# A second MLP's first product over pairs of token tiles by Strassen's scheme, with its token mixes made by scaled stores and accumulating DMAs

## The chip, the cores and the metric

The program runs on one core of a Trainium2 chip. The metric is the device time of one execution in microseconds, as the median of repeated runs.

## What is computed

```python
X = np.fft.fft(np.fft.fft(x, axis=1), axis=2).real   # x: (4, 3072, 256)
h = X @ w_in                                          # (256, 2048)
x = np.maximum(0.01 * h, h) @ w_out                   # (2048, 256): the first MLP
x_prev = the token before, zeros for the first of a batch
xk = mu_k * x + (1.0 - mu_k) * x_prev
xr = mu_r * x + (1.0 - mu_r) * x_prev
k = np.maximum(xk @ w_k, 0.0)                         # w_k: (256, 1024): the first product
v = k * k @ w_v                                       # w_v: (1024, 256)
out = v / (1.0 + np.exp(-(xr @ w_r)))                 # w_r: (256, 256): the gate
```

All is float32. Each matrix product is made of three TensorE products of split operands: with w = wh + wl and x = xh + xl, the kernel adds wh·xh, wl·xh and wh·xl (names that end in h and l, the high and the low part). "High" is a ScalarE copy into the type float32r, "low" is a VectorE subtraction of the high part from the value.

## The kernel before

The tokens of the 4 batches are cut into 24 tiles of 512 (`W`), 6 a batch. A tile's token is a column; the 256 features lie on 128 partitions in two halves, `h` = 0 and 1.

**Transform and first MLP**, to about 889 us of the profiled execution: for each batch the Fourier transform is made from folded input and cosine tables (`fft_mm`), then the loop over `NF` = 16 units of 128 hidden columns for each of 3 pairs of tiles calls `step` (L605): on TensorE `mm_b`, `mm_a` (six products into one bank) and `outmm` (L520, twelve products `o`); on ScalarE and VectorE the evacuation `ev`, `g`, `gh`, `gl`. Two tiles come out at a time, and `flush` copies them out of PSUM (`yo`) and stores them to HBM (`y`), 512 KB by one DMA. In between, the weights of the second MLP are converted in nine pieces (`w2_piece`, five steps each).

**Second MLP**, from about 889 us: for each tile, `load_tile` fetches the tile (`xa`) and, in one to three column runs, the tokens before it (`xb`), by DMAs from SyncE's queue. `prep` makes the mixes: ScalarE scales `xb` (L701, `mt`), VectorE adds the scaled `xa` (L702, `mx`), and `hi_lo` splits the sum (`mh`, `ml`). For each of `NK` = 8 blocks `f` of 128 hidden columns, `k_mm` (L945) makes the first product, six products into a bank `kps` (two feature halves, three split terms each); `k_ev` makes relu and square (`rl` on ScalarE, `k` on VectorE), `k_split` splits the result (`k2h`, `k2l`), and `v_mm` (L986) adds six products to the two banks `v` of the tile. Twice a tile, the gate's six products `rps` (L995) and a sigmoid (`sig`, L997) stand in between. At a tile's end VectorE multiplies `sig` and `v` (`o`, L1004), and the result is stored.

The order on each engine is the order in which the Python program records instructions: there is no scheduler. Each engine takes its list in order; a DMA is issued by the queue of SyncE or, for accumulating ones, of GpSimd (POOL), in order as well. PSUM has eight banks: four of the pool `ps_s` go round, four of `ps_o` hold `v` for two tiles.

Of the kernel before, what the change touches and what calls it, by code (L numbers as in the profile page):

```python
# [17 lines left out]
P = 128  # L18
# [84 lines left out]
def fft_mlp_kernel(ctx, tc, xs, x7, x8, x87, tb, tbs, alt, ce, so, mu, w_in, w_out, w_k, w_v, w_r, out):  # L103
# [5 lines left out]
    yd = [[dram.tile([P, 2, M], F32, name=f"y{b}_{s}") for s in range(2)] for b in range(B)]  # L109
# [279 lines left out]
    omu = misc.tile([P, 4], F32, name="omu")  # L389

# [131 lines left out]

    def flush(b, t, po):
        end = b == B - 1 and t == NT - 1
        for s in range(2):
            if end:
                at = yd[b][s][:, :, t * W:(t + 1) * W]
                yo = stage.tile([P, 2, W], F32, tag="st", bufs=3, name="yo") if s == 0 else None
                for h in range(2):
                    half = yo[:, h] if s == 0 else stage.tile([P, W], F32, tag="h", bufs=2, name="yh")  # L530
                    act_copy(half, po[s][h])
                    if s:
                        Q.dma_start(at[:, h], half)
                if s == 0:
                    Q.dma_start(at, yo)
                continue
            yo = work.tile([P, 2, W], F32, tag="yo", bufs=2, name="yo")
            for h in range(2):
                act_copy(yo[:, h], po[s][h])
            Q.dma_start(yd[b][s][:, :, t * W:(t + 1) * W], yo)  # L540
# [96 lines left out]
    kept = [[dram.tile([P, 2, 256], F32, name=f"w2_{n}{x}") for x in "hl"] for n in range(n_early)]  # L637

# [13 lines left out]
    def w2_piece(n):  # L652
        z = {"fp": stage, "ft": "f"}
        nm, src, at = sources[n]

        def load():
            z["st"] = load_f64(src, 2, 256)

        def parts():
            if n < n_early:  # L660
                return (stage.tile([P, 2, 256], F32R, tag="r", bufs=3, name="wh"),
                        stage.tile([P, 2, 256], F32R, tag="h", bufs=2, name="wl"))
            return at(w2[nm + "h"]), at(w2[nm + "l"])

        head, one, two, low, add, four, five = split_steps(z, 2, 256, parts)

        def last():
            five()
            if n < n_early:
                for k, t in zip(kept[n], z["p"]):  # L670
                    Q.dma_start(k, t.bitcast(F32))
            if n + 1 < len(sources):
                w2_load[n + 1]()
        return load, [lambda: (head(), one()), two, lambda: (low(), add()), four, last]

    w2_load, w2_steps = [], []
    for n in range(len(sources)):
        a, c = w2_piece(n)
        w2_load.append(a)
        w2_steps += c  # L680
# [3 lines left out]
    def load_tile(ti):  # L684
        b, i = tiles[ti]
        s, t = divmod(i, NT)
        p = w2["xp"] if ti == 0 else w2["p2"]
        x = p.tile([P, 2, W], F32, tag="xa", name="xa")
        xprev = p.tile([P, 2, W], F32, tag="xb", name="xb")
        Q.dma_start(x, yd[b][s][:, :, t * W:(t + 1) * W])  # L690
        for s, q, c, n in runs_before(TOKENS[i]):
            if s is None:
                V.memset(xprev[:, :, c:c + n], 0.0)
            else:
                Q.dma_start(xprev[:, :, c:c + n], yd[b][s][:, :, q:q + n])
# [24 lines left out]


    def prep_early(x, xprev, r):
        z = {}

        def mix(h):
            t = stage.tile([P, W], F32, tag="h", bufs=2, name="mt")
            z[h] = stage.tile([P, W], F32, tag="f", bufs=2, name="mx")
            A.activation(t, xprev[:, h], ACTF.Copy, scale=omu[:, h:h + 1])
            V.scalar_tensor_tensor(z[h], x[:, h], mut[:, h:h + 1], t, op0=ALU.mult, op1=ALU.add)

        def split(h):
            if h == 0:
                r["k"] = [stage.tile([P, 2, W], F32R, tag="st", bufs=3, name=f"m{n}") for n in "hl"]
            hi_lo(r["k"][0][:, h], r["k"][1][:, h], z[h])
        return [lambda: mix(0), lambda: mix(1), lambda: split(0), lambda: split(1)]

    tiles = [(b, i) for b in range(B) for i in range(2 * NT)]
    loaded, ready = {}, {}

    def do_prep(ti):  # L740
        x, xprev = loaded.pop(ti)
        ready[ti] = {}
        steps = prep(x, xprev, ready[ti])
        return steps if ti > 0 else prep_early(x, xprev, ready[ti]) + steps[3:]
# [108 lines left out]
    for b in range(B):  # L853
# [5 lines left out]
        for ti in range(0 if b else 1, NT):  # L859
# [3 lines left out]
            for u in range(NF):  # L863
# [9 lines left out]
                step(x, nx)  # L873
                for kb, kind, k_u in ((b, "Pe", pe_u), (b, "Qe", qe_u), (b + 1, "Po", po_u), (b + 1, "Qo", qo_u)):
# [41 lines left out]
                if len(w2_steps) > 5 * (len(sources) - n_early):  # L916
                    if po_u <= i < po_u + 5 or (b > 0 and i < 5):
                        w2_steps.pop(0)()
                elif b == B - 1 and i > 7 and w2_steps and i % 3:
                    w2_steps.pop(0)()  # L920
                if b == B - 1:
                    if i == 33:
                        Q.dma_start(mut, mu)
                    if i == 36:
                        V.tensor_scalar(omu, mut, -1.0, 1.0, op0=ALU.mult, op1=ALU.add)
                        loaded[0] = load_tile(0)
                    if i == 39:
# [20 lines left out]
    def k_ev(ps, r, k2):  # L948
# [3 lines left out]
    def small(tag, dt=F32):  # L952
        return stage.tile([P, W], dt, tag=tag, bufs={"r": 3}.get(tag, 2), name="e" + tag)

    early = []
    for f in range(2):
        early.append([ps_s.tile([P, 512], F32, tag="s", name="ps"), small("h"), small("f")])
        k_mm(early[f][0], f, ready[0]["k"])
        if f == 0:
            step(None, None)  # L960
        k_ev(*early[f])
    kk0 = (small("r", F32R), small("r", F32R))
    hi_lo(*kk0, early[0][2])
    stage_out(hist.pop(0))
    wo.release()
# [4 lines left out]


    p2 = w2["p2"] = ctx.enter_context(tc.tile_pool(name="p2", bufs=2))
    p2.tile([P, 16], F32, tag="pad", bufs=1, name="pad3")

    NB = D // P

    def v_mm(f, kk, vps, end):
        hi, lo = kk
        ws = ((w2["vh"], hi), (w2["vl"], hi), (w2["vh"], lo))
        order = [(i, m, slice(0, W)) for i in range(3) for m in range(NB)]  # L980
        if f == NK - 1:
            halves = [slice(0, W // 2), slice(W // 2, W)] if end else [slice(0, W)]
            order = [(i, m, c) for m in range(NB) for c in (halves if m == NB - 1 else [slice(0, W)]) for i in range(3)]
        for i, m, c in order:
            w, x = ws[i]
            T.matmul(vps[m][:, c], w[:, f, m * P:(m + 1) * P], x[:, c], start=(f == 0 and i == 0),  # L986
                     stop=(f == NK - 1 and i == 2), skip_group_check=c.start > 0)

    def r_mm(xr, sig, m):
        hi, lo = xr  # L990
# [6 lines left out]
        A.activation(sig[:, m], ps, ACTF.Sigmoid)  # L997

    def finish(ti, vps, sig):
        o = p2.tile([P, NB, W], F32, tag="o", name="o")  # L1000
        end = ti == len(tiles) - 1
        for m in range(NB):
            for c in [slice(0, W // 2), slice(W // 2, W)] if end and m == NB - 1 else [slice(0, W)]:
                V.tensor_tensor(o[:, m, c], sig[:, m, c], vps[m][:, c], op=ALU.mult)  # L1004
                if end:
                    Q.dma_start(out[ti, :, m, c], o[:, m, c])
        if ti < len(tiles) - 1:
            Q.dma_start(out[ti], o)
# [140 lines left out]
```

## Time and profile before

| | us |
|---|---|
| median of 3 runs | 1481.06 (1481.03 to 1481.28) |
| profiled execution | 1480.61 |
| its span, first to last instruction | 1478.8 |
| TensorE busy | 1462.4 (99%) |
| VectorE busy | 1008.7 (68%) |
| ScalarE busy | 892.6 (60%) |

The span is 1.8 us shorter than the profiled execution's own time. Busy shares are read together with the chain that ended last: an engine that is busy all the time and carries the chain sets the end; idle time of the others costs nothing. TensorE's instructions overlap: an entry of 389 ns does not mean that the next begins 389 ns later.

### The profile page before, as it was taken

The numbers are of one execution on the slowest core, as the hardware profiler recorded it, in microseconds if no ns is written. First come the engines' busy times: TensorE is split into PE (matmuls) and PEld (weight loads), VectorE is DVE, ScalarE is ACT, GpSimd is POOL, SyncE is SP. The second block draws the span as 40 slices with busy tenths as digits, with TensorE's granted clock in tenths as the row PEclk, the third lists the DMA queues.
The fourth block names the chain that finished last, engine by engine and source line by source line (L and its number), as shares of the span: only waits on it lengthen the run. The fifth ranks groups of instructions, "written<-read, shape, count | busy, mean of one in ns | idle before, by whom it ended". The sixth has DMA issues, their size and how long they took to land.

```text
span 1478.8 us, 17665 instructions
## 1 busy us (share of the span) xinstructions
PE 1462.4 (99%) x6463; PEld 1203.6 (81%) x6463; DVE 1008.7 (68%) x1410; ACT 892.6 (60%) x1473; POOL 124.0 (8%) x145
## 2 busy tenths in 40 slices
PE   6999999999999999999999999999999999999998
PEld 3788888888888888888888888888888888888887
DVE  7886667666676666666667666666666666666665
ACT  4776566656666565665666667555555555556563
POOL 2333100132000222000000000000000000000000
PEclk9999999999999999999999999999999999999999
DMA  8867133654132653142230103212121212121200
GB/s 306 234 162 150 36 100 108 199 105 93 36 122 91 193 103 54 36 158 93 79 80 0 57 1 129 67 62 71 58 71 57 72 58 72 57 72 57 72 29 29
DMA packets 88609, 134.23 MB, mean 91 GB/s; under 512 B 31374, under 2 KB 51863, under 8 KB 84938
## 3 DMA queue, kind: packets, MB, share of 16 engines
q1 hardware_dynamic: 73258, 86.50, 18.5%
q0 software_dynamic: 15264, 46.60, 12.8%
q8 instruction: 50, 0.82, 0.2%
q14 instruction: 37, 0.30, 0.1%
HBM read 105.20 MB, written 27.89 MB: 90 GB/s over the span
## 4 chain that ended last, share of the span: by engine, by line
PE 98%; DVE 1%; ACT 0%; DMA 0%; issue 0%; SPq 0%; POOL 0%; DVEq 0%; POOLq 0%; ACTq 0%
PE o L520 35%; PE v L986 18%; PE kps L945 17%; PE ps L497 9%; PE ps L509 9%; PE rps L995 4%; PE wps L402 1%; PE cps L451 1%; PE dps L553 1%; DMA cet<-in_ce 0%; PE f0Po L310 0%; PE f0Pe L310 0%; PE f2Pe L310 0%; PE f1Pe L310 0%; PE f0Qe L310 0%; PE f3Pe L310 0%
## 5 line engine op out<-in xcount | busy, mean ns | idle before, releaser
L592 DVE SCALAR_TENSOR_TENSOR g<-ev,ps 128x512 f32<-128x512 f32 x192 | 131.6, 685 | 191.9 <-PE ps L509 191.2
L949 ACT ACTIVATE rl<-kps 128x512 f32<-128x512 f32 x190 | 113.5, 597 | 227.8 <-PE kps L945 227.7
L580 DVE TENSOR_TENSOR gl<-g,gh 128x1024 fp32r<-128x1024 f32 x192 | 235.0, 1224 | 4.2 <-ACT gh L129 4.2
L129 ACT ACTIVATE gh<-g 128x1024 fp32r<-128x1024 f32 x192 | 202.7, 1056 | 51.7 <-PE o L520 50.5
L950 DVE SCALAR_TENSOR_TENSOR k<-kps,rl 128x512 f32<-128x512 f32 x190 | 131.3, 691 | 146.2 <-ACT rl L949 145.6
L520 PE MATMUL o<-gh,uoh 128*128 128x512 f32 x768 | 211.9, 390 | 1.0 <-ACT gh L129 1.0
L520 PE MATMUL o<-gl,uoh 128*128 128x512 f32 x768 | 211.2, 389 | 0.1
L520 PE MATMUL o<-gh,uol 128*128 128x512 f32 x768 | 211.1, 389 | 0.0
L132 ACT ACTIVATE g<-ps 128x512 f32<-128x512 f32 x192 | 114.3, 595 | 150.1 <-DVE g L592 149.2
L520 PEld LDWEIGHTS o<-gh,uoh 128*128 128x128 f32 x768 | 144.1, 188 | 32.0 <-ACT gh L129 1.5
L520 PEld LDWEIGHTS o<-gl,uoh 128*128 128x128 f32 x768 | 144.1, 188 | 30.4 <-DVE gl L580 0.5
L520 PEld LDWEIGHTS o<-gh,uol 128*128 128x128 f32 x768 | 144.2, 188 | 30.0
L502 DVE SCALAR_TENSOR_TENSOR ev<-cb,w,ps 128x512 f32<-128x512 f32 x192 | 143.1, 746 | 5.0 <-PE ps L497 2.7
L136 DVE TENSOR_TENSOR k2l<-k,k2h 128x512 fp32r<-128x512 f32 x190 | 129.5, 682 | 0.5 <-ACT k2h L129 0.5
L986 PE MATMUL v<-k2l,wvh 128*128 128x512 f32 x383 | 121.7, 389 | 0.0
L986 PE MATMUL v<-k2h,wvh 128*128 128x512 f32 x383 | 121.7, 389 | 0.0
L986 PE MATMUL v<-k2h,wvl 128*128 128x512 f32 x383 | 121.7, 388 | 0.0
L132 ACT ACTIVATE g<-g 128x512 f32<-128x512 f32 x192 | 119.8, 624 | 1.6 <-DVE g L592 1.6
L129 ACT ACTIVATE k2h<-k 128x512 fp32r<-128x512 f32 x190 | 118.4, 623 | 0.0
L945 PE MATMUL kps<-ml,wkh 128*128 128x512 f32 x380 | 117.1, 389 | 0.0
L945 PE MATMUL kps<-mh,wkh 128*128 128x512 f32 x380 | 117.1, 389 | 0.0
L945 PE MATMUL kps<-mh,wkl 128*128 128x512 f32 x380 | 117.0, 389 | 0.0
(396 smaller groups left out, 2183.1 us busy)
## 6 DMA issues: line engine op xcount, KB each, us to landing
xa<-y SPq DMA_DIRECT2D x24, 512.0 KB
y<-yo SPq DMA_DIRECT2D x23, 512.0 KB
out_dram<-o SPq DMA_DIRECT2D x23, 512.0 KB
tab_a<-in_tbs POOLq DMA_DIRECT2D x8, 1158.0 KB, 6.4
tab_b<-in_tbs POOLq DMA_DIRECT2D x8, 1158.0 KB, 5.6
tab_c<-in_tbs POOLq DMA_DIRECT2D x6, 1158.0 KB, 6.1
tab_d<-in_tbs POOLq DMA_DIRECT2D x6, 1158.0 KB, 6.6
pm<-in_xs POOLq DMA_DIRECT2D x54, 128.0 KB, 3.2
```

The source lines that it names most:

```text
L129: A.activation(o, i, ACTF.Copy)
L132: A.activation(o, i, ACTF.Prelu, alpha=0.01)
L136: V.tensor_tensor(lo, src, hi.bitcast(F32), op=ALU.subtract)
L497: T.matmul(x["ps"], l[:, f], r, start=(i == 0), stop=(i == 2))
L502: V.scalar_tensor_tensor(x["ev"], x["cb"], w128[:, u:u + 1], x["ps"], op0=ALU.mult, op1=ALU.add)
L509: T.matmul(x["ps"], l[:, f], r, start=False, stop=(i == 2), skip_group_check=True)
L520: T.matmul(po[s][h], w[:, u % HF, h * P:(h + 1) * P], g[:, s], start=(u == 0 and i == 0), stop=(u == NF - 1 and i == 2))
L580: V.tensor_tensor(gl, x["g"], x["gh"].bitcast(F32), op=ALU.subtract)
L592: V.scalar_tensor_tensor(x["gt"][:, 1], x["ev"], 2.0, x["ps"], op0=ALU.mult, op1=ALU.subtract)
L945: T.matmul(ps, w[:, k, sl], x[:, k], start=(i == 0), stop=(i == 5))
L950: V.scalar_tensor_tensor(k2, ps, 0.0, r, op0=ALU.max, op1=ALU.mult)
L986: T.matmul(vps[m][:, c], w[:, f, m * P:(m + 1) * P], x[:, c], start=(f == 0 and i == 0), stop=(f == NK - 1 and i == 2), skip_group_check=c ...
```

## The change

For 22 of the 24 tiles the first product is made for two tiles, A and B, and two blocks f0 and f1 at once. With the feature halves 1 and 2 and the weights' 128x128 blocks w(half, block), four results c11 (tile A, f0), c12 (B, f0), c21 (A, f1), c22 (B, f1) need eight block products. Strassen's scheme, in Winograd's form, needs seven (`operands`, products 1 to 7), with three of them accumulated onto the same bank `kx` one after the other: it is read after each (`p1`, `u2`, `u4`, last `c12`). One `superstep` makes the four results; four supersteps (`j` = 0 to 3) make a pair, eleven pairs make 22 tiles. Tiles 0 and 1 keep the old product.

- The combined weights (`ws`, 4 blocks for each two f) are made in two further steps of each of the four pieces of w_k (`combine`, `sum_split`), kept in HBM (`sums`) and loaded back (L1220).
- The combined tokens (`t13`, `t24`) and their splits are made once a pair by `pair_steps`, in the slots `more` of the pair before.
- The mixes are no longer computed in the second MLP. In the first MLP, after each unit, `scale_one` (L526) writes a finished tile's half scaled by mu or 1 - mu to one of four HBM arrays, 256 KB by one DMA: eight stores for each two halves of 128 features of a tile, where one store of 512 KB was. `load_mix` loads the first array's tile by a plain DMA and adds the shifted tokens' runs by accumulating DMAs from GpSimd's queue (L730). The last two tiles are kept unscaled (`yraw`) and scaled in pairs 1 to 4.
- c11 and c21 get relu and square on ScalarE (`eh`, `er`), c22 on VectorE alone, c12 as before. What is left of c21, `late`, is recorded in the next superstep.

```diff
+    def scaled(b, s, t, h, k, y, new):
+        z = new()
+        A.activation(z, y, ACTF.Copy, scale=muts[k][:, h:h + 1])
+        Q.dma_start(yd[k][b][s][:, h, t * W:(t + 1) * W], z)
...
     def flush(b, t, po):
...
-            Q.dma_start(yd[b][s][:, :, t * W:(t + 1) * W], yo)
+            for k in range(4):
+                for h in range(2):
+                    scales.append((b, s, t, h, k, yo[h]))
...
                 step(x, nx)
+                scale_one()
+                if u % 4 == 3:
+                    scale_one()
...
+    def load_mix(dst, k, ti, E=Q):
         b, i = tiles[ti]
         s, t = divmod(i, NT)
...
+        E.dma_start(dst, yd[k][b][s][:, :, t * W:(t + 1) * W])
         for s, q, c, n in runs_before(TOKENS[i]):
...
+            if s is not None:
+                G.dma_start(dst[:, :, c:c + n], yd[k + 1][b][s][:, :, q:q + n], accum_op=ALU.add)
...
+    def operands(z, j):
+        kw = lambda k, f: [w2["k" + x][:, k, f * P:(f + 1) * P] for x in "hl"]
+        sw = lambda n: [w[:, j, n] for w in (wsh, wsl)]
+        half = lambda nm, h: [x[:, h] for x in z[nm]]
+        f0, f1 = 2 * j, 2 * j + 1
+        return {1: (kw(0, f0), half("b", 0)), 2: (kw(1, f0), half("b", 1)), 3: (sw(3), z["b22"]), 4: (kw(1, f1), half("t24", 1)),
+                5: (sw(0), half("t13", 0)), 6: (sw(1), half("t24", 0)), 7: (sw(2), half("t13", 1))}
+
+    def product(ps, wx, start):
+        (wh, wl), (xh, xl) = wx
+        for i, (w, x) in enumerate(((wh, xh), (wl, xh), (wh, xl))):
+            T.matmul(ps, w, x, start=(start and i == 0), stop=(i == 2), skip_group_check=not start)
...
+    def superstep(p, j, z, ta, tb, gates, prep):
...
+        X = bank("kx")
+        product(X, w[1], True)
+        Y = bank("ky")
+        product(Y, w[2], True)
+        p1 = piece("p1", 1)
+        act_copy(p1, X)
+        c = piece("c", 3)
+        V.tensor_tensor(c, p1, Y, op=ALU.add)
+        run_late()
+        if pend:
+            v_mm(pend.pop(0))
+        product(X, w[6], False)
+        Z = bank("kz")
+        product(Z, w[7], True)
+        u2 = piece("u2", 1)
+        act_copy(u2, X)
+        c11["k"] = k_act(c)
+        split_hi(c11)
+        if pend:
+            v_mm(pend.pop(0))
+        product(X, w[5], False)
+        u4 = piece("u4", 1)
+        act_copy(u4, X)
+        split_lo(c11)
+        more(1)
+        for g in gates[:1]:
+            gate_mm(*g)
+        c = piece("c", 3)
+        V.tensor_tensor(c, u4, Z, op=ALU.add)
+        c22["k"] = k_vec(c)
+        if pend:
+            v_mm(pend[0], 0)
+        more(1)
+        for g in gates[:1]:
+            gate_ev(*g)
+        split_hi(c22)
+        product(X, w[3], False)
+        if pend:
+            v_mm(pend.pop(0), 1)
+        split_lo(c22)
+        more(1)
+        product(Z, w[4], False)
+        r = small("h")
+        A.activation(r, X, ACTF.Relu)
+        c12["k"] = small("r")
+        V.scalar_tensor_tensor(c12["k"], X, 0.0, r, op0=ALU.max, op1=ALU.mult)
+        v_mm(c11)
+        split_hi(c12)
+        c = piece("c", 3)
+        V.tensor_tensor(c, u2, Z, op=ALU.add)
+        split_lo(c12)
+        more(9)
...
+            prep[1] += [bh, bl, b22h, b22l]
+            prep[2] += [t13, th, tl, t2]
+            prep[3] += [t4, uh, ul, lambda: r_hi(b), lambda: r_lo(b)]
...
+                prep[j][at:at] = [lambda: scale_one(lambda: small("f"))] * (1 + j // 3)
+            superstep(p, j, za, ta, tb, gates[j:j + 1], prep[j])
```

How the order moves on TensorE, in the middle of the second MLP. Before, one block f of one tile: six products into `kps`, then six for `v`:

```order
L945 MATMUL kps<-mh,wkh 128x512 x2
L945 MATMUL kps<-mh,wkl 128x512 x2
L945 MATMUL kps<-ml,wkh 128x512 x2
L986 MATMUL v_9936<-k2h,wvh 128x512
L986 MATMUL v_9937<-k2h,wvh 128x512
L986 MATMUL v_9936<-k2h,wvl 128x512
L986 MATMUL v_9937<-k2h,wvl 128x512
L986 MATMUL v_9936<-k2l,wvh 128x512
L986 MATMUL v_9937<-k2l,wvh 128x512
```

Now, the beginning of a superstep, from the last of the three instructions of product 1 to product 6:

```order
L1083 MATMUL kx<-bl,wkh 128x512
L1083 MATMUL ky<-bh,wkh 128x512
L1083 MATMUL ky<-bh,wkl 128x512
L1083 MATMUL ky<-bl,wkh 128x512
L1002 MATMUL v_10042<-k2h,wvh 128x512
L1002 MATMUL v_10043<-k2h,wvh 128x512
L1002 MATMUL v_10042<-k2h,wvl 128x512
L1002 MATMUL v_10043<-k2h,wvl 128x512
L1002 MATMUL v_10042<-k2l,wvh 128x512
L1002 MATMUL v_10043<-k2l,wvh 128x512
L1083 MATMUL kx<-t24h,wsh 128x512
```

The bank `kx` is written again nine instructions after product 1 was complete, and ScalarE has to have copied it (`p1`) by then. The whole program has 6276 matrix instructions where it had 6408: 132 fewer.

On ScalarE, before, around two blocks f with the mixes (`mt`, `mh`) between:

```order
L701 ACTIVATE mt<-xb,omu 128x512
L949 ACTIVATE rl<-kps 128x512
L129 ACTIVATE k2h<-k_9387 128x512
L129 ACTIVATE mh<-mx 128x1024
L949 ACTIVATE rl<-kps 128x512
L129 ACTIVATE k2h<-k_9410 128x512
```

Now, from the end of a superstep j = 3 into j = 0 of the next pair:

```order
L1163 ACTIVATE eh<-kx 128x512
L129 ACTIVATE k2h<-er 128x512
L129 ACTIVATE rh<-st 128x1024
L129 ACTIVATE p_11300<-kx 128x512
L1092 ACTIVATE eh<-c 128x512
L1093 ACTIVATE er<-eh 128x512
L129 ACTIVATE k2h<-er 128x512
L129 ACTIVATE u_11325<-kx 128x512
L1092 ACTIVATE eh<-c 128x512
L1093 ACTIVATE er<-eh 128x512
L129 ACTIVATE k2h<-er 128x512
L129 ACTIVATE u_11349<-kx 128x512
```

The copies of `kx` (`p1`, `u2`, `u4`) stand behind chains of three instructions on one value (`eh` relu, `er` square, `k2h` high part), and `p1` of j = 0 stands behind the 1024 wide `rh`.

On GpSimd's queue, which issued nothing in the second MLP, these loads now stand, here a part of one pair (`m` for the first product, `st` for the gate):

```order
L730 DMA m<-y_1_0_69 128x2x255
L730 DMA m<-y_1_0_69 128x2x1
L730 DMA m<-y_1_0_69 128x2x256
L730 DMA st<-y_1_0_85 128x2x255
L730 DMA st<-y_1_0_85 128x2x1
L730 DMA st<-y_1_0_85 128x2x256
```

Each row is one accumulating DMA of one run of columns; a pair has ten of them on average.

## Rows read from the trace of the kernel before

**Rows 1.** the page: busy time by engine; then the chain's shares by engine and line.

```profile
PE 1462.4 (99%) x6463; PEld 1203.6 (81%) x6463; DVE 1008.7 (68%) x1410; ACT 892.6 (60%) x1473; POOL 124.0 (8%) x145
...
PE 98%; DVE 1%; ACT 0%; DMA 0%; issue 0%; SPq 0%; POOL 0%; DVEq 0%; POOLq 0%; ACTq 0%
PE o L520 35%; PE v L986 18%; PE kps L945 17%; PE ps L497 9%; PE ps L509 9%; PE rps L995 4%; PE wps L402 1%; PE cps L451 1%; PE dps L553 1%; DMA cet<-in_ce 0%; PE f0Po L310 0%; PE f0Pe L310 0%; PE f2Pe L310 0%; PE f1Pe L310 0%; PE f0Qe L310 0%; PE f3Pe L310 0%
```

**Rows 2.** busy time by stretch: PE, PEld, DVE, ACT, POOL busy (instructions), clock, DMA share, GB/s.

```profile
0.00:60.00 60.00, 47.80 (x177) 30.12 (x178) 46.97 (x85) 33.79 (x61) 19.75 (x22) 1.00 0.89 291
...
420.00:630.00 210.00, 210.00 (x940) 174.59 (x939) 142.24 (x188) 127.50 (x208) 29.89 (x37) 1.00 0.41 105
...
890.00:900.00 10.00, 10.00 (x45) 8.04 (x44) 6.76 (x10) 7.01 (x12) 0.00 (x0) 1.00 0.95 314
900.00:1100.00 200.00, 200.00 (x884) 165.43 (x883) 137.53 (x199) 120.75 (x199) 0.00 (x0) 1.00 0.19 64
...
1470.00:1479.00 9.00, 4.60 (x24) 3.73 (x22) 2.13 (x4) 0.88 (x2) 0.00 (x0) 0.99 0.17 58
```

**Rows 3.** the chain in order of time, second MLP: start us, us, what.

```profile
1150.89 1.36 PE kps L945 x6
1152.25 1.36 PE v L986 x6
```

**Rows 4.** groups by form: name, shapes xcount | busy us, mean ns | idle before, releasers.

```profile
L945 PE MATMUL kps<-mh,wkh 128*128 128x512 f32 x380 | 117.1, 389 | 0.0
```

**Rows 5.** timeline near the end: start us, us, engine, line, instruction [idle before].

```profile
1462.43 0.60 ACT L949 ACTIVATE rl<-kps 128x512 f32<-128x512 f32 x1 [1.60 <-PE kps L945]
1462.92 0.62 ACT L129 ACTIVATE k2h<-k 128x512 fp32r<-128x512 f32 x1
1463.06 0.69 DVE L950 SCALAR_TENSOR_TENSOR k<-kps,rl 128x512 f32<-128x512 f32 x1 [1.43 <-ACT rl L949]
...
1463.67 0.68 DVE L136 TENSOR_TENSOR k2l<-k,k2h 128x512 fp32r<-128x512 f32 x1
...
1471.24 0.61 PE L995 MATMUL rps<-ml,wrh 128*128 128x512 f32 x2
...
1471.89 0.60 ACT L997 ACTIVATE sig<-rps 128x512 f32<-128x512 f32 x1 [1.60 <-PE rps L995]
...
1472.83 0.19 PEld L986 LDWEIGHTS v<-k2h,wvh 128*128 128x128 f32 x1
```

**Rows 6.** groups by form: ScalarE's and VectorE's other durations.

```profile
L129 ACT ACTIVATE gh<-g 128x1024 fp32r<-128x1024 f32 x192 | 202.7, 1056 | 51.7 <-PE o L520 50.5
...
L701 ACT ACTIVATE mt<-xb,omu 128x512 f32<-128x512 f32 x94 | 67.2, 715 | 0.0
L136 DVE TENSOR_TENSOR ml<-mx,mh 128x1024 fp32r<-128x1024 f32 x47 | 57.6, 1225 | 26.2 <-ACT mh L129 26.2
L129 ACT ACTIVATE mh<-mx 128x1024 fp32r<-128x1024 f32 x47 | 49.4, 1051 | 0.0
...
L1004 DVE TENSOR_TENSOR o<-sig,v 128x512 f32<-128x512 f32 x47 | 30.0, 679 | 2.9 <-PE v L986 2.9
```

**Rows 7.** DMA issues (KB each, us to landing), idle before L230, SyncE's issues at 889 us.

```profile
pm<-in_xs POOLq DMA_DIRECT2D x54, 128.0 KB, 3.2
...
xl<-in_xs POOLq DMA_DIRECT2D x18, 256.0 KB, 5.1
...
  DMA pm<-in_xs: 60.2, 18
...
889.40 1.42 SPq L533 DMA_DIRECT2D y<-yh  x2
```

**Rows 8.** timeline of the last microseconds.

```profile
1474.32 0.28 PE L986 MATMUL v<-k2l,wvh 128*128 128x256 f32 x1
1474.65 1.35 SPq L1006 DMA_DIRECT2D out_dram<-o  x3
```

More of the change, by code (lines that the diff above doesn't have):

```diff
@@ L637, in fft_mlp_kernel @@
     kept = [[dram.tile([P, 2, 256], F32, name=f"w2_{n}{x}") for x in "hl"] for n in range(n_early)]
+    sums = [dram.tile([P, 4, 4, P], F32, name=f"w2s{x}") for x in "hl"]
     def w2_alloc():
@@ L671, in last, with following, sum_last @@
                     Q.dma_start(k, t.bitcast(F32))
+            if nm != "k":
+                following()
+        def following():
             if n + 1 < len(sources):
                 w2_load[n + 1]()
-        return load, [lambda: (head(), one()), two, lambda: (low(), add()), four, last]
+        def sum_last():
+            sum_split()
+            following()
+        return load, [lambda: (head(), one()), two, lambda: (low(), add()), four, last] + ([combine, sum_last] if nm == "k" else [])
     w2_load, w2_steps = [], []
@@ L978, in v_mm, with parts, k_split @@
+    def parts(tag, new, bufs):
+        return [new(tag + x, bufs, F32R) for x in "hl"]
+    def k_split(k2):
+        kk = parts("k2", piece, 4)
+        hi_lo(*kk, k2)
+        return kk
+    def v_mm(x, which=None):
+        t, f, kk = x["t"], x["f"], x["kk"]
         hi, lo = kk
+        if x["first"] and which != 1:
+            t["v"] = [ps_o.tile([P, 512], F32, tag=f"o{t['i'] % 2}{m}", name=f"v{m}") for m in range(NB)]
+        last = x["last"]
+        end = last and t["end"]
         ws = ((w2["vh"], hi), (w2["vl"], hi), (w2["vh"], lo))
-        order = [(i, m, slice(0, W)) for i in range(3) for m in range(NB)]
@@ L981, in v_mm @@
-        if f == NK - 1:
-            halves = [slice(0, W // 2), slice(W // 2, W)] if end else [slice(0, W)]
-            order = [(i, m, c) for m in range(NB) for c in (halves if m == NB - 1 else [slice(0, W)]) for i in range(3)]
-        for i, m, c in order:
[L985 to L990, printed above, removed]
+        full = slice(0, W)
@@ new lines, in v_mm @@
+        if last or which is not None:
+            cols = [slice(0, W // 2), slice(W // 2, W)] if end else [full]
+            order = [(i, m, c) for m in range(NB) if which in (None, m)
+                     for c in (cols if m == NB - 1 else [full]) for i in range(3)]
+        else:
+            order = [(i, m, full) for i in range(3) for m in range(NB)]
+        for i, m, c in order:
+            w, k = ws[i]
+            T.matmul(t["v"][m][:, c], w[:, f, m * P:(m + 1) * P], k[:, c], start=(x["first"] and i == 0),
+                     stop=(last and i == 2), skip_group_check=c.start > 0)
@@ L991, in r_mm, with gate_mm @@
+        if last:
+            for m in range(NB):
+                if which not in (None, m):
+                    continue
+                o = piece("o", 2) if t["i"] % 2 or t["i"] == 0 else small("f")
+                for c in cols if m == NB - 1 else [full]:
+                    V.tensor_tensor(o[:, c], t["sig"][m][:, c], t["v"][m][:, c], op=ALU.mult)
+                    Q.dma_start(out[t["i"], :, m, c], o[:, c])
+    def gate_mm(t, m):
+        hi, lo = t["r"]
         ps = ps_s.tile([P, 512], F32, tag="s", name="rps")
@@ L996, in r_mm @@
                 i += 1
[L997 to L1008, printed above, removed]
@@ new lines, in item, with run_late, k21 @@
+    def item(t, f, first, last):
+        return {"t": t, "f": f, "first": first, "last": last}
+    pend = []
+    late = []
+    def run_late():
+        while late:
+            late.pop(0)()
+    def superstep(p, j, z, ta, tb, gates, prep):
+        w = operands(z, j)
+        bank = lambda n: ps_s.tile([P, 512], F32, tag="s", name=n)
+        more = lambda n=1: [prep.pop(0)() for _ in range(n) if prep]
+        f0, f1 = 2 * j, 2 * j + 1
+        c11, c22 = item(ta, f0, j == 0, False), item(tb, f1, j == 0, False)
+        c12, c21 = item(tb, f0, False, j == 3), item(ta, f1, False, j == 3)
+        X = bank("kx")
[50 more added lines that the diff above has]
+        more(9)
+        def k21():
+            c21["k"] = k_act(c)
+            split_hi(c21)
+            split_lo(c21)
+        late.append(k21)
+        pend.extend([c22, c12, c21])
```

327 lines of the change are left out of this document (185 added, 142 removed).

## The prediction

> **What bounds the kernel now.** Read the page first, then the stretches, then the chain. TensorE is busy for 99% of the span and carries 98% of the chain [rows 1]; the first product alone (`kps`) has 17% of it. By stretch, TensorE fills 210 of 210 us in the first MLP and 200 of 200 in the second; it idles only in the first 60 us and in the tail [rows 2]. The clock is 1.00 (2.4 GHz) throughout. ScalarE and VectorE are busy 121 and 138 of 200 us in the second MLP [rows 2]. The chain in order of time shows what an instruction costs TensorE: six take 1.36 us [rows 3], so 0.227 us each, as do 884 in 200 us [rows 2]. The 389 ns of a group's row [rows 4] is a length with overlap and no price.
>
> **The saving.** A tile's first product has 8 x 6 = 48 instructions; the trace has 380 for each of three forms [rows 4], and 12 under another name make 1152 for 24 tiles. The change leaves two tiles as they are (96) and gives eleven pairs 4 supersteps x 7 products x 3 = 84: 96 + 924 = 1020. That is 132 fewer, x 0.227 = **-29.9 us**, all on the chain. The Trainium skill (TensorE: Matmul & The Clock Gate, section Back-to-back issue gap) gives N/2.4 + 2.5 ns, 215.7 ns for 512 columns; by it the saving would be 28.5 us. The chain here shows 227, and the measurement decides.
>
> **What a superstep asks of the other engines.** It has 21 first-product instructions, 24 for `v` and 6 for the gate: 51 x 0.227 = 11.56 us. Starts that follow closely give the price of an instruction on an engine: ScalarE 0.49 us (`rl` to `k2h`), VectorE 0.61 (`k` to `k2l`) [rows 5], about 0.1 under the rows' lengths; so 0.95 for 1024 columns and 0.61 for a scaled copy on ScalarE, 1.13 for 1024 on VectorE [rows 6]. A dependent instruction costs its length and 0.03: `rl` ends at 1463.03, `k` starts at 1463.06 [rows 5].
> - ScalarE: two chains of relu, square, high part at 3 x 0.65 = 1.96, and seven others at 0.5: 7.4 us. Preparation adds 5.3 us a pair, 1.3 a superstep, and in four pairs the scaled stores 0.6: 9.3 at most of 11.56. Square has no row; I take relu's length, between 0.5 and the 1.06 of an instruction twice as wide [rows 6].
> - VectorE: nine at 0.6, 5.5; outputs 0.6, preparation 2.2: 8.3 of 11.56.
>
> Neither becomes the bound, so TensorE waits only where a single result is late. The removed mixes (`mt`, `mx`, `mh`, `ml`) gave no time while they lay beside TensorE and give none back.
>
> **Where TensorE may wait.** Each copy of `kx` has ten instruction times from the product's last start to the next product's first: 2.27 us. The round trip is 0.42 to the copy's start (the second `rps` instruction starts at 1471.47, `sig` at 1471.89), 0.60 the copy, and 0.22 for the hop and weight load [rows 5]: 1.24. So 1.03 us is left for ScalarE to be late. I walk the seam between j = 3 and j = 0, where most stands in the way; times from the start of j = 3:
> - product 5's last start 5.89, `u4` 6.32; VectorE is then at c11's low part and `t4`, so the sum c22 runs 7.4 to 8.1, relu and square to 8.8, high part to 9.6, low to 10.3, then the 1024 wide `ul`, so `k` of c12 runs 11.35 to 12.04.
> - ScalarE: c12's high part from 12.07, `rh` from 12.59, `p1` 13.53 to 14.13, TensorE ready at 14.35; due at 11.56 + 12 x 0.227 = 14.28. A wait of 0.07. In the four pairs with scaled stores two of these (0.61 each) stand before `uh`, which slips behind c12's high part; the same walk gives 0.3. Together 7 x 0.07 + 4 x 0.3 = 1.7 us.
> - In j = 0 the first product with `v` of the new tile writes a bank that VectorE still multiplies: the old tile's last product starts at 9.29, the output multiplication [rows 6] runs 9.72 to 10.40, TensorE may start at 10.62, due at 10.43. 0.2 x 10 = 2.0 us.
>
> All other copies keep 0.4 to 1.0 to spare by the same walk. Bounds for the waits: 0 (each is smaller than what I left out of the walk) and 0.3 in each of 44 supersteps, 13 us. I take **+3.7**, the walk's.
>
> **The first MLP.** 176 scaled stores of 0.61 us on ScalarE, 1.25 a unit; a unit's 18 instructions take 4.08 us, and ScalarE's three (0.95, 0.49, 0.52) and 0.76 make 2.7. In 420 to 630 us ScalarE is busy for 127.5 of 210 [rows 2], 48 stores of 0.72 bring that to 162. The result `gh` is used a unit later, which is the cover; without it each store would cost its 0.61, 107 us. SyncE issues 154 more DMAs at 0.6 to 0.7 each [rows 7], one in 3.3 us; 256 KB took 5.1 us to land at the worst-placed form [rows 7], and four buffers give 13. Cost 0 to 2 us, taken 0.2: the steps of two more weight pieces may find ScalarE or VectorE waiting for a load once.
>
> **The hand-over at 889 us.** Tile 0's gate and tile 1 need accumulated loads whose buffers come free only here, when DMA is at 0.95 of its time already [rows 2]. Tile 1's first: its plain load is about the sixth issue (4 us), lands after some 5, then GpSimd's sixth accumulation issues and lands, 5.1 [rows 7], and the split takes 2.3: some 16 us. Tile 0's six remaining blocks cover 6 x 2.72 = 16.3. Cost 0 to 5 us, taken 0.5. The tail (last matrix instruction 1474.32, store 1474.65 [rows 8]) keeps its shape; 0 to 0.5, taken 0.3.
>
> **Sum**: -29.9 + 3.7 + 0.2 + 0.5 + 0.3 = -25.2 on the profiled execution's 1480.61 gives 1455.4; it stands 0.45 below the median of the runs, so **1456** in round numbers from 1481.06 - 25.2 = 1455.9.
>
> **Rivals.**
> 1. *TensorE waits in every superstep.* If square or the chains run longer than relu's row, `u2` and `u4` eat the spare 1.03 and the sums c follow late. For it: ScalarE goes from 60% busy to some 80%, and each late result moves the next, since c21 runs into the following superstep. Against: the spare at each copy. At 0.25 to 0.45 a superstep it takes back 11 to 20 us in place of 3.7: 1463 to 1472 (1481.06 - 25.2 - 3.7 + 11 or 20).
> 2. *The accumulating loads come late, and the kernel is slower.* A pair's tokens `m` have one buffer and are loaded at the pair's start, five accumulations behind two plain loads; their first reader `bh` stands in j = 1, some 20 us later. In the kernel before, the third and fourth accumulation onto one tile waited, 60.2 us in 18 times [rows 7]. If the five waited for one another at 5.1 us each and the first for its plain load, 5 + 26 = 31 us, the pair is 11 us late: ten pairs, 1566. It decides from 2.5 us late a pair (25.2 / 10), a chain of about 22.5 us. Against: the runs touch different columns, so none needs the other, and 3.2 to 5.1 us then pass side by side.
> 3. *The clock falls.* In the first 60 us TensorE is busy for only 47.8 and the granted clock is 1.00 [rows 2], which speaks against it. At 1.2 GHz a superstep takes 11.56 us more; from 2.2 of the 44 (25.2 / 11.56) the gain is gone, and half of them would give 1456 + 254 = 1710. The Trainium skill (TensorE: Matmul & The Clock Gate, section A second HAM failure mode: psum-queue depth-cycling) says that small idles between groups that cycle through PSUM banks made the clock swing in one kernel; by that rule this is what short waits at `kx` would do, and the stretch at the start shows idles without it.
>
> **How the numbers follow.** Forecast 0.76, with its own range 1451 (no wait at all: 1481.06 - 29.9 = 1451.2) to 1462; rival 1 0.16; rival 2 0.04; rival 3 0.02; 0.02 for a sum of small delays that ends within 3 us of before. A measurement of this kernel tells 0.2% (3 us) from no change. Faster by more than that: 0.76 + 0.16 + 0.01 (rival 2 at a small delay) = 0.93; the same 0.02; slower 0.05. The range runs from 1451 to 1466, which takes in the first part of rival 1 and leaves some 0.17 outside.
>
> **What would show it.** Right: TensorE 6276 matrix instructions, still over 97% busy; pairs of 46.2 to 46.8 us in the chain; its idle time a few us, at `kx` (waiting for `p1`) and `v` (waiting for the output multiplication); clock 1.00 from the first MLP on. Wrong: idle at `kx` over 10 us in all (rival 1), TensorE or ScalarE waiting for `m` or `st` (rival 2), a granted clock under 1 after 60 us (rival 3), or waits in the first MLP of more than 2 us.

## The result, and the profile after

The changed kernel takes 1459.82 us (median of 4 runs, 1459.43 to 1460.42) against 1481.05 of the kernel before on the same chip: ratio 0.9859, 95% interval 0.9842 to 0.9876. It is faster, inside the range, 3.8 us above the forecast of 1456. The profiled execution took 1459.6 us with a span of 1457.5, 21.3 less than before.

The page's line of busy times and the chain's shares by engine, which answer to [rows 1]:

```profile
PE 1437.1 (99%) x6331; PEld 1178.1 (81%) x6331; DVE 1025.9 (70%) x1429; ACT 1070.5 (73%) x1771; POOL 256.6 (18%) x265
...
PE 88%; ACT 5%; DVE 4%; DMA 1%; issue 1%; POOL 0%; SPq 0%; ACTq 0%; DVEq 0%; POOLq 0%
```

TensorE has 132 instructions fewer (6463 - 6331), as the saving asks. The chain now leaves TensorE for ScalarE and VectorE in places, since it follows every wait back to what caused it. (Ahead of the prediction the program is said to have 6276 matrix instructions where it had 6408; the trace has 6331 and 6463, the same difference.) The busy times by stretch (columns as in [rows 2]) show where time goes:

```profile
420.00:630.00 210.00, 210.00 (x941) 174.65 (x940) 143.60 (x193) 155.32 (x257) 29.22 (x37) 1.00 0.54 152
889.00:905.00 16.00, 15.54 (x67) 12.22 (x66) 5.16 (x8) 5.30 (x10) 7.68 (x9) 1.00 1.04 303
905.00:907.00 2.00, 0.00 (x0) 0.00 (x0) 0.00 (x0) 0.98 (x2) 2.00 (x5) 1.00 1.37 179
907.00:909.00 2.00, 1.88 (x6) 1.19 (x7) 1.90 (x3) 1.38 (x4) 2.00 (x5) 0.75 1.27 173
909.00:912.00 3.00, 3.00 (x10) 2.40 (x9) 2.74 (x4) 2.98 (x4) 3.00 (x6) 0.60 1.13 172
912.00:1100.00 188.00, 187.50 (x823) 153.65 (x822) 138.40 (x195) 145.82 (x239) 42.90 (x39) 1.00 0.65 147
```

The first MLP is full (210 of 210), with ScalarE at 155.3 where it was 127.5. At the hand-over TensorE stands for 2 us and more, and then, though it is "busy" all the time, does fewer matmuls than fit: the view counts 10 in the 3 us from 909 on, where it counts 15 in the full stretches of e1 below. The granted clock (the column after POOL) is 0.75 and 0.60 there. In the pairs TensorE loses little. The timeline of the hand-over names the cause:

```profile
890.40 0.53 SPq L727 DMA_DIRECT2D t24h<-y  x1
...
896.75 1.07 POOL L730 DMA_DIRECT2D t24h<-y  x1 [54.22 <-DMA t24h<-y]
898.40 2.18 POOL L730 DMA_DIRECT2D t24h<-y  x2 [0.57 <-issue]
...
903.91 0.63 PE L937 MATMUL kps<-ml,wkh 128*128 128x512 f32 x2
...
906.01 1.06 ACT L129 ACTIVATE rh<-t24h 128x1024 fp32r<-128x1024 f32 x1 [5.83 <-DMA t24h<-y]
...
907.12 0.73 PE L1019 MATMUL rps<-rh,wrh 128*128 128x512 f32 x2 [2.59 <-ACT rh L129]
...
908.38 1.22 PE L1019 MATMUL rps<-rl,wrh 128*128 128x512 f32 x2
909.40 1.05 PE L1002 MATMUL v<-k2h,wvh 128*128 128x512 f32 x2
```

Tile 0's gate tokens (`t24h`) are loaded from 890.40 on; GpSimd's three accumulations follow from 896.75, and the last lands just before `rh` starts at 906.01, 15.6 us after the first issue. TensorE would have come to the gate at 904.37 (two matmuls of 0.23 after 903.91) and has nothing to do until `rh` is there. Then two matmuls take 0.86 us (909.40 to the next pair at 910.26), 0.43 each in place of 0.227: the level of 1.2 GHz. Summed over the matmuls' starts, all that exceeds 0.227 us between 889 and 940 us is 4.6 us: 2.76 of standing and 1.85 behind it, nearly all of it slow matmuls. In the pairs the same sum is 3.8 us. -29.9 + 4.6 + 3.8 = -21.5, and the span fell by 21.3.

The chain in order of time shows the 3.8 (from a pair of the first four, then from a later one):

```profile
1031.82 0.49 ACT p L129
...
1032.35 0.96 PE kx L1083 x3
...
1040.13 1.53 PE v L1002 x6
...
1153.07 1.36 PE rps L1019 x6
...
1164.63 1.36 PE rps L1019 x6
...
1172.79 0.78 PE kx L1083 x3
...
1180.39 1.52 PE v L1002 x6
```

A superstep without a wait takes 1164.63 - 1153.07 = 11.56 us. In later pairs the third product of j = 0 takes 0.78 in place of 0.68 us and a second-product block 1.52 in place of 1.36: 0.24 us a pair (with the rounding of the chain's rows). In the first four pairs `kx` also starts 0.33 us late, 0.585 in all. 4 x 0.585 + 6 x 0.24 = 3.8.

### The profile page after: what moved, and what is told of

Read it like the earlier page. It is cut to its first block, busy times and chain, and to the rows that moved or that the text cites. A ratio compares the mean times of both kernels' runs of the same rounds, so it can differ in the third digit from the quotient of the medians.

```text
span 1457.5 us, 18081 instructions
## 1 busy us (share of the span) xinstructions
PE 1437.1 (99%) x6331; PEld 1178.1 (81%) x6331; DVE 1025.9 (70%) x1429; ACT 1070.5 (73%) x1771; POOL 256.6 (18%) x265
## 4 chain that ended last, share of the span: by engine, by line
PE 88%; ACT 5%; DVE 4%; DMA 1%; issue 1%; POOL 0%; SPq 0%; ACTq 0%; DVEq 0%; POOLq 0%
PE o L521 36%; PE v L1002 14%; PE ps L510 9%; PE ps L498 9%; PE kx L1083 6%; PE rps L1019 3%; PE kz L1083 3%; PE ky L1083 1%; ACT k2h L129 1%; PE wps L403 1%; DMA t24h<-y 1%; PE kps L937 1%; DVE er L1087 1%; DVE er L1165 1%; DVE k2l L1101 1%
## 5 line engine op out<-in xcount | busy, mean ns | idle before, releaser
L129 ACT ACTIVATE gh<-g 128x1024 fp32r<-128x1024 f32 x192 | 201.9, 1052 | 12.8 <-PE o L521 10.2
L1101 DVE TENSOR_TENSOR k2l<-er,k2h 128x512 fp32r<-128x512 f32 x176 | 121.7, 691 | 110.2 <-ACT k2h L129 105.7
L129 ACT ACTIVATE k2h<-er 128x512 fp32r<-128x512 f32 x176 | 111.2, 632 | 74.6 <-DVE er L1165 58.5
L1002 PE MATMUL v<-k2h,wvh 128*128 128x512 f32 x383 | 129.0, 393 | 0.0
L1002 PE MATMUL v<-k2h,wvl 128*128 128x512 f32 x383 | 127.6, 390 | 0.0
L1002 PE MATMUL v<-k2l,wvh 128*128 128x512 f32 x383 | 127.3, 389 | 0.0
L730 POOL DMA_DIRECT2D st<-y x54 | 62.3, 1804 | 184.3 <-DMA st<-y 144.5
L730 POOL DMA_DIRECT2D m<-y x54 | 61.7, 1871 | 166.5 <-DVE er L1165 123.0
L1002 PEld LDWEIGHTS v<-k2h,wvh 128*128 128x128 f32 x383 | 72.2, 188 | 17.7 <-DVE ef L1010 3.0
L1002 PEld LDWEIGHTS v<-k2l,wvh 128*128 128x128 f32 x383 | 72.2, 188 | 15.1
L1002 PEld LDWEIGHTS v<-k2h,wvl 128*128 128x128 f32 x383 | 72.2, 188 | 14.7
```

Source lines behind the costliest of these rows:

```text
L129: A.activation(o, i, ACTF.Copy)
L730: G.dma_start(dst[:, :, c:c + n], yd[k + 1][b][s][:, :, q:q + n], accum_op=ALU.add)
L1002: T.matmul(t["v"][m][:, c], w[:, f, m * P:(m + 1) * P], k[:, c], start=(x["first"] and i == 0), stop=(last and i == 2), skip_group_check=c ...
L1101: V.tensor_tensor(x["kk"][1], x["k"], x["kk"][0].bitcast(F32), op=ALU.subtract)
```

## The experiments

Gaps, below, are what the spacings of TensorE's matmul starts exceed 0.227 us by, summed over a stretch of a run's trace (spacings up to 0.25 us left out). Diffs are against the changed kernel; `...` marks what is left out of them.

### The hand-over

**e1: the gate tokens earlier.**

```diff
-                y = (stage if end else work).tile([P, 2, W], F32, tag="st" if end else "yo", bufs=3 if end else 2, name="yo")
+                y = (w2["xp"] if end else work).tile([P, 2, W], F32, tag="xa" if end else "yo", bufs=1 if end else 2, name="yo")
...
+                        x0r = stage.tile([P, 2, W], F32, tag="st", bufs=3, name="x0r")
+                        load_mix(x0r, 2, 0)
...
-    t0["xr"] = load_one("t24h", 2, 0)
+    t0["xr"] = x0r
```

> Edit: tile 0's gate tokens are loaded some 20 us sooner, into the third st buffer (the last output tile of the first MLP then goes through xa). Theory A (one late chain): in the changed kernel TensorE idles 2.76 us near 905 us because rh waits for the last of six accumulations onto t24h, and the matmuls after it start 427 ns apart for some 3 us, 1.85 us more; without the late chain both go: 1459.8 - 4.6 = 1455.2 us, no granted clock under 1 near 905 us. Rival B (the queues are full at the hand-over whatever is loaded): tile 1's tokens take the place of tile 0's gate tokens, land near 906 us as those did, the split takes 2.3 us, and the first product of tile 1, due near 907 us, waits 1 to 2 us: 1456 to 1458 us, with a clock under 1 after that wait.

Measured: 1454.84 us (1453.44 to 1455.59). (The three accumulations were taken for six in this text.) By stretch:

```profile
903.00:906.00 3.00, 3.00 (x15) 2.43 (x14) 2.37 (x3) 2.39 (x5) 3.00 (x5) 1.00 1.25 177
906.00:909.00 3.00, 3.00 (x15) 2.49 (x14) 1.34 (x3) 2.24 (x3) 1.64 (x2) 1.00 1.06 223
```

No idle time, clock 1.00, gaps 0 between 889 and 940 us, though the DMA share is still over 1. Theory A; the full queues alone cost nothing.

**e2: without the accumulations.**

```diff
-            if s is not None:
+            if s is not None and acc:
...
-    t0["xr"] = load_one("t24h", 2, 0)
+    t0["xr"] = load_one("t24h", 2, 0, acc=False)
```

> Leaves out part of the computation: the accumulating DMAs onto tile 0's gate tokens (t24h), so its gate is computed without the previous tokens' share; the plain load stays. Theory A (the accumulations are what is late): the plain load landed near 896 us, 10 us before it is read, so the idle of 2.76 us and the slow matmuls behind it (1.85 us) go: 1455.2 us. Rival B (the transfers of the hand-over share a full DMA, whatever their kind): the plain load or tile 1's tokens still come late, and 1 to 2.8 us of idle stay: 1456 to 1459 us.

Measured: 1455.66 us (1454.6 to 1456.63), gaps 0 at the hand-over. The gate starts 3 us sooner than at 907.12 and without an idle time before it:

```profile
904.08 0.63 PE L1019 MATMUL rps<-rh,wrh 128*128 128x512 f32 x2
```

The plain load alone is in time; what is late are the accumulations, the first of which waits until it has landed (the row at 896.75 above).

**e9: the gap filled.**

```diff
+                if g == 0 and x is t0:
+                    spare = ps_s.tile([P, 512], F32, tag="s", name="spare")
+                    k_mm(spare, f, xk)
+                    k_mm(spare, f, xk)
```

> Adds twelve first-product matmuls into a bank that nobody reads, just ahead of tile 0's gate: 12 x 0.227 = 2.72 us of work in the 2.76 us in which TensorE idles. Theory A2 (the granted clock falls to 1.2 GHz because TensorE has idled): the clock stays at 1.00, the slow matmuls (1.85 us) go: 1459.8 - 1.85 = 1458.0 us. Rival C (the clock falls for another reason, such as the DMA load at that time): the clock still falls near 908 us, and the time stays at 1459.8. Rival D (the gap isn't at that place): the time rises by 2.7 to 1462.5 us.

Measured: 1458.08 us (1456.64 to 1458.58). The timeline and a stretch:

```profile
906.76 0.63 PE L937 MATMUL spare<-ml,wkh 128*128 128x512 f32 x2
907.23 0.62 PE L1019 MATMUL rps<-rh,wrh 128*128 128x512 f32 x2
```

```profile
906.00:909.00 3.00, 3.00 (x14) 2.39 (x14) 2.28 (x3) 2.37 (x4) 3.00 (x6) 1.00 1.34 188
```

The gate starts when it did (907.23 against 907.12), but with TensorE busy until then the clock stays at 1.00, and 1.74 us are gained by twelve matmuls that nobody needs. DMA is as busy as before (a share of 1.34 here, 1.27 there), so the clock fell after the idle time, not for the traffic.

### The saving and the pace of a superstep

**e3: an eighth product.**

```diff
+        product(Y, w[2], False)
         product(Z, w[4], False)
```

> Adds the eighth product back as time, not as mathematics: three more matmuls onto ky in each superstep, so the output is not the reference's. Theory A (TensorE sets the pace of a superstep): 132 x 0.227 = 29.9 us more, less the 3.8 us of waits in the pairs, which the 0.68 us of more room at each copy take away: 1459.8 + 26.1 = 1485.9 us, pairs of 49 us. Rival (the supersteps have TensorE time to spare, since ScalarE or VectorE sets their pace): some of the three hide in waits, 1460 to 1480 us.

Measured: 1484.16 us (1483.88 to 1486.29), 24.3 more than the changed kernel. (`ky` has been read by then, so nothing that is computed depends on the added products; the expectation is wrong there.) From the chain in order of time:

```profile
1161.46 1.36 PE rps L1019 x6
...
1173.70 1.36 PE rps L1019 x6
```

A superstep takes 12.24 us = 54 x 0.227, and the pairs have no gap left. 29.9 - 3.8 of waits is 26.1; the hand-over's gaps are 4.1 here in place of 4.6, which leaves 25.6, and the profiled execution was about 0.9 us earlier than that of the changed kernel when it reached them. TensorE sets the pace.

**e4: one more copy on ScalarE.**

```diff
+        act_copy(small("f"), X)
         u2 = piece("u2", 1)
```

> Adds one 512-wide ScalarE copy, which nobody reads, ahead of each u2: 44 x some 0.6 us. Theory A (each copy of kx has 1.03 us to spare, and only the seam from j = 3 to j = 0 is at its limit): u2 itself keeps 0.4 us; p1 of j = 0 comes 0.6 us later in ten pairs, +6 us; the other copies, with 0.4 to 1.0 to spare by the walk, lose 0 to 0.2 each, +0 to 6 us: 1466 to 1472 us, TensorE idle 0.9 us a pair at the seam. Rival (ScalarE already sets the pace of every superstep): 44 x 0.6 = +26 us, 1486 us. Rival (nothing is near its limit, the 3.8 us of waits are chance): 1460 us.

Measured: 1469.97 us (1468.58 to 1470.77), +10.2; gaps in the pairs 13.4 us. A seam from the chain:

```profile
1175.88 1.04 ACT rh L129
1176.93 0.49 ACT p L129
...
1177.46 0.96 PE kx L1083 x3
```

`kx` starts 1.07 us after the matmul before it: the idle time sits at the seam, behind `rh` and `p1`, 1.07 to 1.24 us of spacing in every pair, and elsewhere there are few long gaps. 44 copies of 0.6 us would be 26. Theory A; a superstep has room for one more copy, its seam none.

**e5: stores out of j = 3.**

```diff
+    def load_y(n):
...
-                prep[j][at:at] = [lambda: scale_one(lambda: small("f"))] * (1 + j // 3)
+            if p < 5 and j == 3:
+                load_y(p)
+            at, n = ((0, 2), (7, 1), (1, 1), (0, 0))[j]
+            if p < 5:
+                prep[j][at:at] = [lambda: scale_one(lambda: small("r"))] * n
```

> Takes the scaled stores out of j = 3 in the first four pairs: two in j = 0, one in j = 1, one in j = 2, from a buffer of their own and into the r buffers. Theory A (the stores ahead of uh make the seam late): TensorE's waits in these pairs fall from 0.585 us, as they stand in the changed kernel, to the 0.24 of the later pairs: 4 x 0.345 = 1.4 us, 1459.8 - 1.4 = 1458.4 us. Rival (ScalarE is late at the seam wherever in the pair the stores stand, since each chain hands its delay on): the waits stay at 0.5 to 0.6 a pair, 1459.8 us.

Measured: 1458.76 us (1457.46 to 1460.98); the time cannot tell. Its trace can. The chain, to be held against 0.96 and 1.53 above:

```profile
1034.30 0.94 PE kx L1083 x3
...
1042.05 1.53 PE v L1002 x6
```

The start of `kx` is late by 0.14 us in place of 0.33, the rest stays: 0.39 a pair in place of 0.585, gaps in the pairs 3.0 us in place of 3.8. So the stores ahead of `uh` were more than half of the late start, not all of it.

**e6: by output bank.**

```diff
+            if x["first"] and t["i"] > 1:
+                order = sorted(order, key=lambda z: z[1])
```

> Orders the six matmuls of the first second-product block of a tile by output bank (three onto bank 0, then three onto bank 1; before, they alternate), so bank 1 is written first 0.45 us later. Theory A (these matmuls wait for the output multiplication that still reads the bank): start gaps of 262 and 337 ns in place of 227 go, 0.145 us x 10 pairs = 1.45 us: 1458.4 us; if the wait for bank 0 (0.035) stays, 1458.7. Rival (the wait only moves to the next copy of kx, where ScalarE is as late): 1459.8 us, and longer waits at kx.

Measured: 1457.5 us (1456.95 to 1458.41). In the chain:

```profile
1031.23 0.96 PE kx L1085 x3
...
1039.00 1.36 PE v L1004 x6
```

The block takes 1.36 us again and the seam is as before; gaps in the pairs fall from 3.8 to 2.3. (Of the 2.3 us by which the median fell, 1.0 is not the edit's: in the profiled executions the hand-over's gap begins that much sooner, at 903.2 against 904.1.) Theory A: the wait was for the bank that VectorE's output multiplication reads.

### What lies beside TensorE

**e8: tokens a superstep later.**

```diff
-            m = load_k(p + 1)
+            m = Later()
...
+            if not end and j == 1:
+                m.m = load_k(p + 1)
```

> Loads the next pair's tokens (two plain loads, five accumulations) one superstep, 11.56 us, later. Theory A (in the changed kernel a pair's last accumulation lands 17.8 us after the first issue and its first reader bh stands 21.8 us after, so 4 us of cover): bh is late by some 7.5 us, TensorE idles 6 to 7.5 us in each of ten pairs: +60 to 75 us, and if each such idle is followed by slow matmuls as at the hand-over (1.85 us), +19 more: 1520 to 1554 us. Rival (the loads are much faster when nothing waits for them, the 17.8 us are only the order of issue): under 10 us more, below 1470 us.

Measured: 1483.42 us (1480.15 to 1486.13), +23.6: both missed. The timeline, once around 1105 and once around 1205 us:

```profile
1105.73 1.06 ACT L129 ACTIVATE bh<-m 128x1024 fp32r<-128x1024 f32 x1 [1.92 <-DMA m<-y]
...
1111.10 0.64 PE L1083 MATMUL kx<-t24h,wsh 128*128 128x512 f32 x1 [1.88 <-ACT p L129]
...
1193.53 1.18 SPq L727 DMA_DIRECT2D m<-y  x2
...
1205.64 1.06 ACT L129 ACTIVATE bh<-m 128x1024 fp32r<-128x1024 f32 x1 [2.42 <-DMA m<-y]
...
1210.44 0.50 PE L1083 MATMUL kx<-t24h,wsh 128*128 128x512 f32 x1 [1.81 <-ACT p L129]
```

`bh` reads the first tile of the pair alone, and that is there 1205.64 - 1193.53 = 12.1 us after the first issue; the 17.8 us of the expectation were the last accumulation of the second tile, which is read later. The cover in the changed kernel is thus some 21.7 - 12.1 = 9.6 us in the first pairs, not 4 (later pairs have `bh` 24.7 us after the first issue), and 11.56 us of delay leave TensorE waiting 17.4 us in all for `p1`. The stretches after the two idles:

```profile
1111.00:1115.00 4.00, 3.90 (x10) 3.11 (x11) 1.46 (x3) 3.87 (x8) 0.00 (x0) 0.57 0.63 199
...
1210.00:1214.00 4.00, 3.56 (x16) 2.95 (x17) 2.32 (x4) 3.87 (x8) 0.00 (x0) 1.00 0.67 115
```

After 1.88 us of idle the clock fell, after 1.81 it did not. Three of the ten pairs show slow matmuls.

**e10 and e11: each scaled store of the first MLP twice.** In e10 both copies go to the same place, in e11, whose edit this is in part, the added one goes to memory of its own (`spare`; e10 has the added line without it):

```diff
...
         if scales:
+            if scales[0][0] < B - 1 or scales[0][2] < NT - 1:
+                scaled(*scales[0], new, spare)
             scaled(*scales.pop(0), new)
```

> Makes each of the 176 scaled stores of the first MLP twice (copy and DMA). In the changed kernel ScalarE's busy time in 420 to 630 us rose by 27.8 us for 48 stores, to 155.3 of 210, and TensorE lost nothing. Theory A (they lie in the cover of a unit, 4.08 us, of which ScalarE needs 2.7 without them; by busy time alone there is room for twice as many, 183 of 210): 1459.8 us, at most 2 more. Rival (the cover is the order of ScalarE's instructions, not its busy time: 2.5 stores a unit bring a unit to 2.7 + 1.45 = 4.15 us, and gh, a unit ahead, falls behind): 0.07 us x 70 units = 5 us at least, and up to 0.58 for each of the 176 added, 102 us: 1465 to 1562 us.

Measured, e10: 1599.73 us, above both. The waits, of SyncE's queue and of ScalarE (us in total, times, longest):

```profile
SPq L527 <- DMA y<-ys: 482.5, 176, 8.2
```

```profile
ACT ys L526 <- DMA y<-ys: 117.9, 71, 7.1
```

The edit brought a wait of its own: the second store of each two waits for the first, which writes the same place, and ScalarE waits for the buffers behind it. That says nothing of the cover, so e11 keeps the two copies apart:

> The 176 scaled stores of the first MLP twice, as in the run before, but the second copy goes to memory of its own that nobody reads. In the run before, SyncE waited 482.5 us in 176 times for the first of the two stores to land, since both wrote the same place, and ScalarE 117.9 us for the buffers behind it; that was a wait of the edit's own. Theory A (only ScalarE's busy time counts, 155.3 of 210 us, 183 with twice as many): 1459.8 to 1462 us. Rival (order counts: 2.5 stores a unit bring ScalarE to 2.7 + 1.45 = 4.15 us in a unit of 4.08): 0.07 us x 70 units = 5 us at least, and up to 0.58 for each of the 176 added, 102 us: 1465 to 1562 us, TensorE waiting for gh. If the four buffers were what failed in the run before, ScalarE still waits for y<-ys here and the time stays near 1600 us.

Measured, e11: 1505.68 us (1505.2 and 1506.15), +45.9. Its waits, and the stretch that answers to the one from 420 us above:

```profile
DVE gl L595 <- ACT gh L129: 48.1, 47, 4.3
ACT ys L526 <- DMA w<-ys: 34.1, 20, 6.7
...
PE ps L510 <- DVE ev L503: 23.5, 14, 5.3
```

```profile
420.00:630.00 210.00, 201.72 (x889) 165.57 (x888) 135.73 (x184) 172.97 (x288) 29.36 (x37) 0.99 0.68 210
```

ScalarE is busy for 173 of 210 us and still TensorE loses time, so theory A is out. The time lies in the rival's range, at 0.26 us a store, but not by its sum: the prediction's 2.7 us a unit hold 1.25 stores already, so 2.5 stores make 2.0 + 1.5 = 3.5 us in a unit of 4.08. What the waits show is that ScalarE stands for the four store buffers (34.1 us for the added copies and 6.9 for the others; none in the changed kernel), that VectorE waits for ScalarE's late results (`gl` for `gh`), and that TensorE waits for `ev`, which stands behind such waits on VectorE. So the last guess of the expectation names the wait, with far too high a price. A run with more buffers was not made, so it is not shown that they are the only cause. One set of stores lies in the cover, a second does not, long before ScalarE is full.

**e7: joined.** e1, e5 and e6 together.

> Joins the early load of tile 0's gate tokens, the stores moved out of j = 3 and the order by bank. From the three runs' traces, as TensorE's start gaps over 227 ns: hand-over 4.6 -> 0 us; output-bank gaps 0.145 x 10 = 1.45 -> 0; seam in the first four pairs 0.44 -> 0.25 each, 0.8 us in all. 1459.8 - 4.6 - 1.45 - 0.8 = 1453.0 us, if the parts don't touch each other (theory A). Rival: TensorE, early by 1.45 us at ten places, waits that much longer at the next copy of kx: 1454.5 us.

Measured: 1452.56 us (1451.78 to 1453.76), ratio to the kernel before 0.9816 (0.9803 to 0.9829), 7.3 us under the changed kernel. The stretches that answer to those of the changed kernel:

```profile
905.00:907.00 2.00, 2.00 (x11) 1.65 (x10) 1.98 (x3) 1.97 (x4) 1.15 (x2) 1.00 0.84 209
...
912.00:1100.00 188.00, 188.00 (x828) 154.69 (x827) 140.70 (x198) 149.34 (x247) 41.39 (x38) 1.00 0.63 151
```

The parts add: 1.6 us of gaps are left in the pairs, none at the hand-over.

## Why the prediction was right, point by point

- **The saving**, -29.9 us: right. 132 instructions are gone, and e3 puts their price back. The rate of 0.227 us holds at 11.56 us for 51 and 12.24 for 54. (The prediction asked for 6276 instructions in the trace; 6463 - 132 is 6331, and that is what is there.)
- **Waits in the supersteps**, +3.7: 3.8. The split is nearly right too: at the seam 0.10 and 0.44 us in place of 0.07 and 0.3 (six seams and four, where the prediction counts seven and four), at the output bank 0.145 in place of 0.2. Errors in both directions cancel here, so the closeness of the sum is in part luck. Pairs take 46.9 us behind the stores and 46.5 later, against 46.2 to 46.8. e6 shows the bank, e4 and e5 the seam. Only the stores' share in the first four pairs is less than the walk's 0.23, as e5 left 0.14 of the late start.
- **The first MLP**, +0.2: none to be seen; TensorE is full. e11 shows that this cover is limited.
- **The hand-over**, +0.5 with bounds 0 to 5: **4.6**, and this is the whole of the miss. Three things failed in the step. It walked tile 1's tokens and not tile 0's gate, whose tokens are issued one load sooner but are read sooner still. It had 16.3 us of cover, six whole blocks; but the gate stands ahead of the sixth block's second product, and TensorE comes to it at 904.37, 14.0 us after its tokens' first issue at 890.40. They need 16.7 us: 6.35 until GpSimd issues the first accumulation, behind the plain load, 2.4 more until it issues the third, 6.7 until that lands (6.6 to 6.8 for the three, not the 3.2 to 5.1 of [rows 7]), 1.3 until `rh` is made and the gate starts. The difference is the 2.76 us of standing. And the step had no term for the clock, 1.85 us. e1 and e2 show the accumulations as the cause, e9 the price of the clock. That 4.6 lies inside the bounds is in part luck: they were made for other tokens and without the clock.
- **The tail**, +0.3: about 0; it keeps its shape.
- **Rival 1** (a wait in every superstep): no. Square takes 0.63 us, as taken, and e4 shows that one more copy fits.
- **Rival 2** (accumulating loads late): the mechanism is real, but its place is the hand-over. In the pairs `bh` never waits; e8 gives the cover, 9.6 us.
- **Rival 3** (the clock falls): it did, in one place, for some 3 us after an idle of 2.6 us. The prediction named a granted clock under 1 after 60 us as a sign of being wrong; it came true there, and cost 1.85 us. Short waits didn't bring it about: in e4 ten spacings of 1.07 to 1.24 us, one a pair, left the clock where it was.

  The rule of the Trainium skill (TensorE: Matmul & The Clock Gate, section A second HAM failure mode: psum-queue depth-cycling) is that small idles between groups of matmuls, coming often, make the clock swing. The waits of e4 did not do so, but they stand some 47 us apart; no run here has them as often, so the rule itself is not tested.

## What to carry to other kernels

Where a stage begins, walk the loads in the order in which they are issued to the first reader of each, and give an accumulating load its full chain: plain load, then the accumulations behind it. Price an idle of TensorE of some 2.5 us or more with the slow matmuls that may stand after it; here they added two thirds to it. An engine's busy share overstates the room on it: with its stores doubled, ScalarE gave out at 173 of 210 us, waiting for the buffers of its stores.

## What the runs showed of the hardware

- After a stand of TensorE the granted clock fell to 1.2 GHz for some 3 us: in the hand-overs of the changed kernel and of e3 to e6 and e8 (2.55 to 3.6 us from one matmul's start to the next, 4.1 to 5.1 us lost in all) and in three pairs of e8 (2.27, 2.98 and 3.00 us). After 2.20 us or less it never did in these runs, the first 60 us of the kernel before among them, where the longest such spacing is 1.6. But in e11 it stayed after 2.5, 2.6 and 4.0 us, and in e10 after 2.8, so the length of the stand alone does not decide; what else does is open. With matmuls that nobody needs in the gap it stayed at 2.4 GHz (e9).
- Accumulating DMAs that stand one behind the other on GpSimd's queue are issued at one in 1.1 us: at the hand-over of the changed kernel the eight from 898.40 on start 0.73 to 0.83 us apart and end 1.1 apart, so the length of an entry grows from 1.08 to 3.66 us. The mean of 1.8 us over the 54 onto `st` holds that queueing; the first onto `t24h`, alone, took 1.07.
- Where two stores go to the same place, SyncE's queue waited for the first before it issued the second: 482.5 us in 176 times, 2.7 us each (e10).
